# A two-layer attention and dense kernel: another order and another place of operands in the second product, and sums over the keys for two row tiles together

## Chip, cores and metric

The kernel runs on one core of a Trainium2 chip. The metric is the device time of one execution in microseconds (us); the median of three runs is given. The profile is that of one further execution. TensorE multiplies matrices, VectorE (DVE), ScalarE (ACT) and GpSimd (POOL) work element by element, SyncE (SP) issues the transfers.

## The reference

The input x has 2048 rows of D = 576 numbers. Twice in turn a linear attention and a dense block are added to it, each on a layer norm of x:

```python
qkv = x @ wqkv                                   # 32 heads of 18
phi_q = cat(softmax(q @ w_phi), softmax(-(q @ w_phi)))      # per head, 36 features
phi_k = cat(softmax(k @ w_phi), softmax(-(k @ w_phi)))
kv  = einsum("bhsf,bhsd->bhfd", phi_k, v)        # sums over all rows (keys)
z   = einsum("bhsf->bhf", phi_k)
o   = (phi_q @ kv) / (phi_q @ z + 1e-6)
x   = x + o @ wo
h   = relu(layernorm(x) @ w1 + b1) ** 2          # 576 -> 4608
x   = x + h @ w2 + b2                            # 4608 -> 576
```

All is in 32-bit floating point.

## The kernel before

**Tiling.** The rows are cut into NB = 4 blocks of TB = 512, each block into NT = 4 row tiles of P = 128. The 4608 hidden features are cut into NF = 36 slices of 128. For large products an operand is held as two parts, a high part (rounded to fp32r by ScalarE) and a low part (the difference, by VectorE or GpSimd); a product is then high x high + low x high + high x low. Such a product is one pass of TensorE per pair of parts.

**The dense block of a single block of rows** (`g_mlp`, from L1093; two blocks in each layer, so four in all). `first(f)` loads a slice of w1 and of w2 (r1, r2), splits them (h1 and l1; s2), and takes a PSUM tile ph. `hidden(f)` runs 14 matmuls of 512 columns into ph (L1135). `square(f)` makes the squares on ScalarE and their low part on VectorE (hh, hl in the tile hb, which begin SK = 48 numbers, 192 bytes, into it). The second product has two kinds of matmul. `by_rows` (L1162) handles the first R = D - P = 448 output columns: squares of one row tile are the weights, w2's first 448 columns are the moving operand, and each row tile t has its own accumulator acc[t]. `features` (L1153) handles the last 128 output columns the other way round: w2's last 128 columns are the weights, 512 squares are the moving operand, and the accumulator acc[KC] is transposed at the end. `second(f)` runs, for slice f, 12 matmuls of the first kind and 3 of the second. A step of the loop is first(f + 1), hidden(f), square(f), second(f - 1).

The tile s2 holds r2's high part in columns 0 to 575 and its low part in columns 576 to 1151: within a low or high part the first 448 columns are for by_rows, the last 128 for features. It is filled by one activation (L1114) and two subtractions (L1119 on VectorE, L1120 on GpSimd). It has room for 1440 columns.

**The pair of blocks** (`g_pair`, from L1380). The other two blocks of a layer go through the hidden product together, by a scheme of seven products for two slices (`product`, L1461, weights made by `split_pair`). For the first of the two the second product runs in between (`products`: by_rows L1493, features L1483); the squares of the second are kept in memory and its second product comes at the end (`seconds`). Here `second` already runs all 12 row matmuls and then the three of the features. `load_wide` (L1449 to L1451) fills s2 as above.

**The sums over the keys.** `kv_tile` (L670) adds one row tile's share of kv and z into a PSUM tile kvp that lives through a layer: for each of the 32 heads a matmul with 32 columns of values as weights in a 128 x 32 part of the array and 36 moving columns (L686); the profile counts two matmuls for each, 64 for a row tile. It reads the values (tiles of four slots, `next_slot`) and the softmaxes e (buffers of the tag "E", four of them). In layer 0 `g_keys` makes values, keys and softmaxes tile by tile for three blocks and sums a tile when two newer ones are waiting (`pending`); the last two of them are summed in `g_k` by `then`. In layer 1 `back_keys` makes the keys of two blocks beside `seconds` of layer 0 (`late` holds what isn't summed yet: a tile is summed when one newer one waits, the last one when the next block starts), and after it a third block's tiles are summed one by one behind their values (`lagged`, L1888). The last block's four tiles are summed in `barrier` (L1667): `keys()` makes the values of tile t + 2 and sums tile t, and between its steps the query softmaxes (`softs`) and the queries of another block go on.

**Order.** The program's text gives priorities: within a basic block a scheduler at compile time puts each engine's instructions in order by their place in the text and by when buffers and operands are ready; `tc.issue_after` pins some behind others. `weave` puts steps of one generator between those of another by costs written in the program. A tile's buffer is given to the next tile of its tag when the last reader is done.

Of the kernel before, what the change touches and what calls it, by code (L numbers as in the profile page):

```python
# [7 lines left out]
F32 = mybir.dt.float32  # L8
# [13 lines left out]
def layers_kernel(  # L22
# [42 lines left out]
    NS = H // NQ  # L65
    PAD = 32
    SK = 48
    assert VW <= 32 and NS == HG + 1 and NG == NQ + 1

    cst = ctx.enter_context(tc.tile_pool(name="cst", bufs=1))  # L70
# [28 lines left out]
    def drain(gen):  # L99
        for _ in gen:  # L100
            pass
# [655 lines left out]
    def g_k(x, pair, es, name, then=None, ready=None):  # L757
        raws = []
        for t in range(NT):
            for i in range(t, min(t + 2, NT)):  # L760
                if i == len(raws):
                    raws.append(make_raw(x, i, pair, f"{name}k"))
                    yield
            if ready and t == 2:
                ready()
            with tc.issue_after(dense["split", 0].ins) if ready and t == 2 else nullcontext():
                es.append(soft_k(raws[t], f"{name}K{t}"))
            if then and t:
                then(t - 1)
            yield  # L770
        if then:
            yield
            then(NT - 1)
            yield
# [318 lines left out]
    def g_mlp(layer, b, x, after, name, rest=None, then=None):  # L1093
# [7 lines left out]
        def first(f, early=False):  # L1101
            cols = slice(f * P, (f + 1) * P)
            r1 = sb.tile([P, NC, P], F32, tag="r1", name=f"{name}r1_{f}")
            r2 = sb.tile([P, D], F32, tag="r2", name=f"{name}r2_{f}")
            nc.sync.dma_start(r1[:, :KC], w1[: KC * P, cols].rearrange("(c p) n -> p c n", p=P))
            load_twice(r1[:, KC], w1, f * P, P)
            nc.sync.dma_start(r2, w2[cols])
            hl1 = sb.tile([P, NC * HP], F32R, tag="h1", name=f"{name}h1_{f}")
            h1 = hl1[:, : NC * P].rearrange("p (c n) -> p c n", n=P)
            l1 = hl1[:, NC * P : 2 * NC * P].rearrange("p (c n) -> p c n", n=P)  # L1110
            s2 = sb.tile([P, NC * HP], F32R, tag="s2", name=f"{name}s2_{f}")
            with tc.issue_after(dense["turn", 2 * f + 1].ins) if early else nullcontext():
                nc.scalar.activation(h1, r1, AF.Copy)
            nc.scalar.activation(s2[:, :D], r2, AF.Copy)  # L1114
            with tc.issue_after(dense["scaled1"].ins) if early else nullcontext():
                dense["lowered"] = (nc.gpsimd if early else nc.vector).tensor_sub(l1, r1, h1.bitcast(F32))

            def low():
                nc.vector.tensor_sub(s2[:, D : D + R], r2[:, :R], s2[:, :R].bitcast(F32))  # L1119
                nc.gpsimd.tensor_sub(s2[:, D + R : 2 * D], r2[:, R:], s2[:, R:D].bitcast(F32))  # L1120

            if early:
                lows.append(low)
            else:
                low()
            ph = wtile(f"{name}ph{f}") if f == 1 else ps_a.tile([P, TB], F32, tag="h", name=f"{name}ph{f}")
            parts[f] = (h1, l1, s2, ph)
# [19 lines left out]

        def features(f, ks):
            s2, hh, hl = parts[f]
            hi, lo = s2[:, R:D], s2[:, D + R : 2 * D]  # L1150
            for k in ks:
                a, m = ((hi, hh), (lo, hh), (hi, hl))[k]
                nc.tensor.matmul(acc[KC], a, m, start=(f == 0 and k == 0), stop=(f == NF - 1 and k == 2))  # L1153

        def by_rows(f, ts, ks):
            s2, hh, hl = parts[f]
            hi, lo = s2[:, :R], s2[:, D : D + R]
            for t in ts:
                rows = slice(t * P, (t + 1) * P)
                for k in ks:  # L1160
                    a, m = ((hh, hi), (hh, lo), (hl, hi))[k]
                    nc.tensor.matmul(acc[t][:, :R], a[:, rows], m, start=(f == 0 and k == 0),  # L1162
                                     stop=(f == NF - 1 and k == 2))

        def second(f):

            for ks in ((0, 1), (2,)):
                by_rows(f, range(NT), ks)
                features(f, ks)
            del parts[f]  # L1170

        every = slice(0, TB)
# [207 lines left out]
    def g_pair(layer, blocks, x, after, name):  # L1380
# [61 lines left out]
        def load_wide(f):  # L1442
            if f >= NF and f % 2:
                r2 = sb.tile([P, NC, P], F32, tag="r1", name=f"{name}r2_{f}").rearrange("p c n -> p (c n)")[:, :D]
            else:
                r2 = sb.tile([P, D], F32, tag="r2", name=f"{name}r2_{f}")
            nc.sync.dma_start(r2, w2[(f % NF) * P : (f % NF + 1) * P])
            s2 = sb.tile([P, NC * HP], F32R, tag="h1" if f >= NF and f % 2 else "s2", name=f"{name}s2_{f}")
            nc.scalar.activation(s2[:, :D], r2, AF.Copy)  # L1449
            nc.vector.tensor_sub(s2[:, D : D + R], r2[:, :R], s2[:, :R].bitcast(F32))  # L1450
            nc.gpsimd.tensor_sub(s2[:, D + R : 2 * D], r2[:, R:], s2[:, R:D].bitcast(F32))  # L1451
            wide[f] = s2

        def product(k, ps, key, op, start):
# [22 lines left out]
        def features(f, ks):  # L1477
            b, g = divmod(f, NF)
            s2, (hh, hl) = wide[f], high[f]
            hi, lo = s2[:, R:D], s2[:, D + R : 2 * D]  # L1480
            for k in ks:
                a, m = ((hi, hh), (lo, hh), (hi, hl))[k]
                nc.tensor.matmul(accs[b][KC], a, m, start=(g == 0 and k == 0), stop=(g == NF - 1 and k == 2))  # L1483

        def by_rows(f, ts, ks):
            b, g = divmod(f, NF)
            s2, (hh, hl) = wide[f], high[f]
            hi, lo = s2[:, :R], s2[:, D : D + R]
            for t in ts:
                rows = slice(t * P, (t + 1) * P)  # L1490
                for k in ks:
                    a, m = ((hh, hi), (hh, lo), (hl, hi))[k]
                    nc.tensor.matmul(accs[b][t][:, :R], a[:, rows], m, start=(g == 0 and k == 0),  # L1493
                                     stop=(g == NF - 1 and k == 2))
# [172 lines left out]
    def barrier(layer, b, prev, x, xprev, kes, vpair, qpair):  # L1667
# [13 lines left out]
        def keys():  # L1681
            for t in range(NT):
                if t + 2 < NT:
                    vts.append(make_v(x, t + 2, vpair, f"{n}"))
                with tc.issue_after(ahead[0].ins) if ahead else nullcontext():
                    kv_tile(layer, vts[t], kes[t], f"{n}{t}")
                yield

        softs = g_soft(raws, er, f"{n}f", 2)
# [55 lines left out]
    keep_split("k", kpair)  # L1745
    pending = []

    def g_keys(b):
        for t in range(NT):
            vt = make_v(xT[b], t, vpair, f"v0_{b}")  # L1750
            raw = make_raw(xT[b], t, kpair, f"k0_{b}")
            yield
            e = soft_k(raw, f"K0_{b}_{t}")
            if len(pending) > 1:
                kv_tile(0, *pending.pop(0))
            pending.append((vt, e, f"kv0_{b}_{t}"))
            yield
        if b < NB - 2:
            spill(b, xT[b])

    for b in range(NB - 1):
# [2 lines left out]
    load_biases()  # L1764
    kes = []
    qpair = []
    drain(g_k(xT[NB - 1], kpair, kes, f"k0_{NB - 1}", then=lambda t: pending and kv_tile(0, *pending.pop(0)),
              ready=lambda: qpair.extend(wpair("q", "t0", TAGS_B))))

    order = [NB - 1, NB - 2] + list(range(NB - 2))  # L1770
# [2 lines left out]
    for layer in range(2):  # L1773
# [24 lines left out]
        def back_keys():  # L1798
            new_slots("vs")
            late, ahead = [], []  # L1800
            normed = {b: {} for b in order[:3]}

            def norm_of(b):
# [3 lines left out]
            for i, b in enumerate(order[:3]):  # L1807
# [8 lines left out]
                    if n > 5:  # L1816
                        next(loads, None)
                drain(loads)
                while late:
                    kv_tile(1, *late.pop(0))  # L1820
                    yield 0.8
                if not last:
                    spill(b, xk)
                    norm = norm_of(order[i + 1])
# [18 lines left out]
                        raw_half(t, half)  # L1843

                def start(t):
                    es[t] = soft_parts(raws.pop(t), f"k{m}K{t}")

                def end(t):
# [3 lines left out]
                def keep_sums(t):  # L1852
                    if not last:
                        late.append((vts[t], es[t], f"kv{m}_{t}"))
                        if len(late) > 1:
                            kv_tile(1, *late.pop(0))

                for t in range(2):
                    raw_half(t, 0)
# [23 lines left out]
        if layer == 0:  # L1883

            prev, b = order[-2], order[-1]
            spare["tags"] = ["acc0", "acc1", "acc2", "acc3", "h"]
            x, xprev, vpair = {}, keep["x"], keep["v"]
            weave(lagged(NT, lambda t: make_v(xprev, t, vpair, "v1_prev"),  # L1888
                         lambda t, vt: kv_tile(1, vt, keep["es"][t], f"kv1_prev{t}")),
                  g_norm(lambda t: rows[t], x, "n1_last"), 1.0)  # L1890
            kpair = wpair("k", "w1_last", TAGS_B)
            kes = []
            qpair = []
            drain(g_k(x, kpair, kes, "k1_last", ready=lambda: qpair.extend(wpair("q", "t1", TAGS_B))))
            order = [b, prev] + order[:2]
# [22 lines left out]
```

## Time and profile before

| | before |
|---|---|
| median of three runs | 2455.33 us (2454.56 to 2456.44) |
| profiled execution, its own time | 2458.63 us |
| its span, first to last instruction | 2456.9 us |
| granted TensorE clock | 1.000 |
| matmuls in the profile | 15110 |
| DMA traffic | 348.67 MB, mean 142 GB/s |

PE is TensorE's matmuls, PEld its loads of weights. In the timeline a line has the start in us, the time to the end of the last instruction of a group, the engine, the line of the kernel, operation, output tile <- input tiles, shape of weights, shape of the moving operand and the number of instructions. A name such as m_3acc is block 3's accumulator; m_p stands for the pair, t0 for the barrier of layer 0. Matmuls are pipelined, so the time of one (362 or 389 ns) is longer than the distance between the starts of two, and that distance is the cost of one in a stream. In the groups by shape a line ends with the busy time in us and mean ns of one, then the idle time of the engine before it and what ended that.

### The profile page before, as it was taken

The numbers are of one execution on the slowest core, as the hardware profiler recorded it, in microseconds if no ns is written. First come the engines' busy times: TensorE is split into PE (matmuls) and PEld (weight loads), VectorE is DVE, ScalarE is ACT, GpSimd is POOL, SyncE is SP. The second block draws the span as 40 slices with busy tenths as digits, with TensorE's granted clock in tenths as the row PEclk, the third lists the DMA queues.
The fourth block names the chain that finished last, engine by engine and source line by source line (L and its number), as shares of the span: only waits on it lengthen the run. The fifth ranks groups of instructions, "written<-read, shape, count | busy, mean of one in ns | idle before, by whom it ended". The sixth has DMA issues, their size and how long they took to land. (4 is left out here: it accounts for less than half of the span.)

```text
span 2456.9 us, 41466 instructions
## 1 busy us (share of the span) xinstructions
PE 2444.1 (99%) x15110; PEld 2168.8 (88%) x15110; DVE 1534.4 (62%) x2503; ACT 1261.0 (51%) x2243; POOL 967.4 (39%) x1117
## 2 busy tenths in 40 slices
PE   9999999999999999999999999999999999999999
PEld 8999888889888888888999998888888888888898
DVE  7778939464866655545766787584547665555454
ACT  4344545443546766664433445554445466666643
POOL 4455303212335565542433442132122455565322
PEclk9999999999999999999999999999999999999999
DMA  9224533356434433338753154333573444433364
GB/s 325 72 73 165 164 101 98 102 162 218 135 119 139 146 109 107 112 101 299 252 190 143 54 173 121 104 98 114 159 242 94 128 137 146 122 96 118 114 198 129
DMA packets 248891, 348.67 MB, mean 142 GB/s; under 512 B 30126, under 2 KB 155950, under 8 KB 246126
## 3 DMA queue, kind: packets, MB, share of 16 engines
q1 hardware_dynamic: 247428, 344.66, 44.6%
q8 instruction: 118, 1.93, 0.3%
q10 hardware_dynamic: 1258, 1.37, 0.2%
q14 instruction: 87, 0.71, 0.1%
HBM read 280.93 MB, written 65.00 MB: 141 GB/s over the span
## 5 line engine op out<-in xcount | busy, mean ns | idle before, releaser
L1451 POOL TENSOR_TENSOR m_ps<-m_pr,m_ps 128x128 fp32r<-128x128 f32 x144 | 122.1, 848 | 317.5 <-ACT m_ps L1449 262.3
L1450 DVE TENSOR_TENSOR m_ps<-m_pr,m_ps 128x448 fp32r<-128x448 f32 x144 | 101.2, 703 | 181.4 <-ACT m_ps L1449 181.4
L1493 PE MATMUL m_pacc<-m_ps,m_phb 128*128 128x448 f32 x864 | 185.1, 362 | 0.0
L1493 PEld LDWEIGHTS m_pacc<-m_ps,m_phb 128*128 128x128 f32 x864 | 161.9, 188 | 14.7
L1449 ACT ACTIVATE m_ps<-m_pr 128x576 fp32r<-128x576 f32 x144 | 98.3, 683 | 119.6 <-issue 68.0
L1493 PE MATMUL m_pacacc<-m_ps,m_phc 128*128 128x448 f32 x648 | 147.2, 365 | 0.0
L1493 PEld LDWEIGHTS m_pacacc<-m_ps,m_phc 128*128 128x128 f32 x648 | 119.4, 188 | 7.9
L1162 PE MATMUL m_2acc<-m_2s,m_2hb 128*128 128x448 f32 x432 | 99.6, 364 | 0.0
L1162 PE MATMUL m_0acc<-m_0s,m_0hb 128*128 128x448 f32 x432 | 99.5, 364 | 0.0
L1162 PE MATMUL m_3acc<-m_3s,m_3hb 128*128 128x448 f32 x432 | 98.9, 364 | 0.0
L1162 PE MATMUL m_1acc<-m_1s,m_1hb 128*128 128x448 f32 x432 | 98.9, 364 | 0.0
L1135 PE MATMUL m_2ph<-a_2nh,m_2h 128*128 128x512 f32 (+1 forms) x380 | 97.4, 383 | 0.1
L1135 PE MATMUL m_0ph<-a_0nh,m_0h 128*128 128x512 f32 (+1 forms) x380 | 97.3, 383 | 0.1
L1135 PE MATMUL m_1ph<-t1onh,m_1h 128*128 128x512 f32 (+1 forms) x380 | 96.8, 382 | 0.0
L1135 PE MATMUL m_3ph<-t0onh,m_3h 128*128 128x512 f32 (+1 forms) x380 | 96.8, 382 | 0.0
L1162 PEld LDWEIGHTS m_2acc<-m_2s,m_2hb 128*128 128x128 f32 x432 | 80.9, 188 | 10.1 <-ACT m_2hb L1143 0.2
L1162 PEld LDWEIGHTS m_0acc<-m_0s,m_0hb 128*128 128x128 f32 x432 | 80.9, 188 | 10.0 <-ACT m_0hb L1143 0.2
L1162 PEld LDWEIGHTS m_3acc<-m_3s,m_3hb 128*128 128x128 f32 x432 | 81.0, 188 | 9.8
L1162 PEld LDWEIGHTS m_1acc<-m_1s,m_1hb 128*128 128x128 f32 x432 | 81.0, 188 | 9.8
L1120 POOL TENSOR_TENSOR m_3s<-m_3r,m_3s 128x128 fp32r<-128x128 f32 x36 | 25.0, 696 | 161.4 <-ACT m_3s L1114 154.0
L1120 POOL TENSOR_TENSOR m_1s<-m_1r,m_1s 128x128 fp32r<-128x128 f32 x36 | 25.3, 704 | 160.5 <-ACT m_1s L1114 145.8
L1135 PEld LDWEIGHTS m_1ph<-t1onh,m_1h 128*128 128x128 f32 x380 | 68.7, 188 | 13.8 <-DVE t1onh L517 0.2
(2448 smaller groups left out, 7294.6 us busy)
## 6 DMA issues: line engine op xcount, KB each, us to landing
m_pr<-in_B_w SPq DMA_DIRECT2D x144, 288.0 KB
m_pr<-in_B_w SPq DMA_DIRECT2D x72, 256.0 KB
hd<-m_pu SPq DMA_DIRECT2D x72, 256.0 KB
m_pg<-hd SPq DMA_DIRECT2D x72, 256.0 KB
m_3r<-in_B_w SPq DMA_DIRECT2D x36, 288.0 KB
m_2r<-in_B_w SPq DMA_DIRECT2D x36, 288.0 KB
m_1r<-in_B_w SPq DMA_DIRECT2D x36, 288.0 KB
m_0r<-in_B_w SPq DMA_DIRECT2D x36, 288.0 KB
```

The lines of the kernel that those rows point to most:

```text
L1120: nc.gpsimd.tensor_sub(s2[:, D + R : 2 * D], r2[:, R:], s2[:, R:D].bitcast(F32))
L1135: dense["hidden"] = nc.tensor.matmul(ph[:, cols], a, m, start=(k == 0), stop=(k == len(ops) - 1))
L1162: nc.tensor.matmul(acc[t][:, :R], a[:, rows], m, start=(f == 0 and k == 0), stop=(f == NF - 1 and k == 2))
L1449: nc.scalar.activation(s2[:, :D], r2, AF.Copy)
L1450: nc.vector.tensor_sub(s2[:, D : D + R], r2[:, :R], s2[:, :R].bitcast(F32))
L1451: nc.gpsimd.tensor_sub(s2[:, D + R : 2 * D], r2[:, R:], s2[:, R:D].bitcast(F32))
L1493: nc.tensor.matmul(accs[b][t][:, :R], a[:, rows], m, start=(g == 0 and k == 0), stop=(g == NF - 1 and k == 2))
```

## The change

In s2 the parts are set out anew: rows' high part at column 0, rows' low part at 448, features' high part at FC = 2 x 448 + 48 = 944, features' low part at 1072. The activation that filled the high part becomes two. `second` of `g_mlp` runs the features' three matmuls together behind all twelve of the rows. And kv_tile is called for two row tiles together: in `g_keys` when three are waiting, in `g_k` for both that are left, in `barrier` and for the third block of layer 1 behind every second tile; in `back_keys` all that is waiting, which by the order of its pipeline is four tiles when the next block starts.

```diff
+    FC = 2 * (D - P) + SK
...
-            nc.scalar.activation(s2[:, :D], r2, AF.Copy)
+            nc.scalar.activation(s2[:, :R], r2[:, :R], AF.Copy)
+            nc.scalar.activation(s2[:, FC : FC + P], r2[:, R:], AF.Copy)
...
-                nc.vector.tensor_sub(s2[:, D : D + R], r2[:, :R], s2[:, :R].bitcast(F32))
-                nc.gpsimd.tensor_sub(s2[:, D + R : 2 * D], r2[:, R:], s2[:, R:D].bitcast(F32))
+                nc.vector.tensor_sub(s2[:, R : 2 * R], r2[:, :R], s2[:, :R].bitcast(F32))
+                nc.gpsimd.tensor_sub(s2[:, FC + P : FC + 2 * P], r2[:, R:], s2[:, FC : FC + P].bitcast(F32))
...
-            hi, lo = s2[:, R:D], s2[:, D + R : 2 * D]
+            hi, lo = s2[:, FC : FC + P], s2[:, FC + P : FC + 2 * P]
...
-            hi, lo = s2[:, :R], s2[:, D : D + R]
+            hi, lo = s2[:, :R], s2[:, R : 2 * R]
...
             for ks in ((0, 1), (2,)):
                 by_rows(f, range(NT), ks)
-                features(f, ks)
+            features(f, range(3))
```

The same edits of s2, features and by_rows stand in `g_pair`. The sums:

```diff
                 with tc.issue_after(ahead[0].ins) if ahead else nullcontext():
-                    kv_tile(layer, vts[t], kes[t], f"{n}{t}")
+                    for i in (t - 1, t) if t % 2 else ():
+                        kv_tile(layer, vts[i], kes[i], f"{n}{i}")
...
+    def sum_pending():
+        for _ in range(min(2, len(pending))):
+            kv_tile(0, *pending.pop(0))
...
-            if len(pending) > 1:
-                kv_tile(0, *pending.pop(0))
+            if len(pending) > 2:
+                sum_pending()
...
-    drain(g_k(xT[NB - 1], kpair, kes, f"k0_{NB - 1}", then=lambda t: pending and kv_tile(0, *pending.pop(0)),
+    drain(g_k(xT[NB - 1], kpair, kes, f"k0_{NB - 1}", then=lambda t: sum_pending(),
...
-                while late:
-                    kv_tile(1, *late.pop(0))
-                    yield 0.8
+                if late:
+                    sum_late()
+                    yield 1.6
...
                 def start(t):
+                    if len(late) > 1:
+                        sum_late()
                     es[t] = soft_parts(raws.pop(t), f"k{m}K{t}")
...
                     if not last:
                         late.append((vts[t], es[t], f"kv{m}_{t}"))
-                        if len(late) > 1:
-                            kv_tile(1, *late.pop(0))
...
-            weave(lagged(NT, lambda t: make_v(xprev, t, vpair, "v1_prev"),
-                         lambda t, vt: kv_tile(1, vt, keep["es"][t], f"kv1_prev{t}")),
-                  g_norm(lambda t: rows[t], x, "n1_last"), 1.0)
+            def prev_sums():
+                made = {}
+                for t in range(NT + 1):
+                    if t < NT:
+                        made[t] = make_v(xprev, t, vpair, "v1_prev")
+                    for i in (t - 2, t - 1) if t and t % 2 == 0 else ():
+                        kv_tile(1, made.pop(i), keep["es"][i], f"kv1_prev{i}")
+                    yield
+
+            weave(prev_sums(), g_norm(lambda t: rows[t], x, "n1_last"), 1.0)
```

`sum_late` sums all that `late` holds.

More of the change, by code (lines that the diff above doesn't have):

```diff
@@ L1448, in load_wide @@
             s2 = sb.tile([P, NC * HP], F32R, tag="h1" if f >= NF and f % 2 else "s2", name=f"{name}s2_{f}")
-            nc.scalar.activation(s2[:, :D], r2, AF.Copy)
-            nc.vector.tensor_sub(s2[:, D : D + R], r2[:, :R], s2[:, :R].bitcast(F32))
-            nc.gpsimd.tensor_sub(s2[:, D + R : 2 * D], r2[:, R:], s2[:, R:D].bitcast(F32))
+            nc.scalar.activation(s2[:, :R], r2[:, :R], AF.Copy)
+            nc.scalar.activation(s2[:, FC : FC + P], r2[:, R:], AF.Copy)
+            nc.vector.tensor_sub(s2[:, R : 2 * R], r2[:, :R], s2[:, :R].bitcast(F32))
+            nc.gpsimd.tensor_sub(s2[:, FC + P : FC + 2 * P], r2[:, R:], s2[:, FC : FC + P].bitcast(F32))
             wide[f] = s2
@@ L1479, in features @@
             s2, (hh, hl) = wide[f], high[f]
-            hi, lo = s2[:, R:D], s2[:, D + R : 2 * D]
+            hi, lo = s2[:, FC : FC + P], s2[:, FC + P : FC + 2 * P]
             for k in ks:
@@ L1487, in by_rows @@
             s2, (hh, hl) = wide[f], high[f]
-            hi, lo = s2[:, :R], s2[:, D : D + R]
+            hi, lo = s2[:, :R], s2[:, R : 2 * R]
             for t in ts:
@@ L1800, in back_keys, with sum_late @@
             late, ahead = [], []
+            def sum_late():
+                while late:
+                    kv_tile(1, *late.pop(0))
             normed = {b: {} for b in order[:3]}
```

## The prediction

> **What bounds the kernel now.** I read the page first, for the engines' shares.
>
> ```profile
> span 2456.9 us, 41466 instructions
> PE 2444.1 (99%) x15110; PEld 2168.8 (88%) x15110; DVE 1534.4 (62%) x2503; ACT 1261.0 (51%) x2243; POOL 967.4 (39%) x1117
> ```
>
> TensorE is busy all the time, and the next engine has a third of its time free. A change gains here only by what it takes out of TensorE's stream, and loses only by what holds that stream up. Busy says little about speed, so I went to the timeline of TensorE, where the distance from one start to the next is the cost of a matmul. One step of a block that runs alone (hidden product of one slice of features, second product of the slice before):
>
> ```profile
> 420.71 1.31 PE L1135 MATMUL m_3ph<-t0onh,m_3h 128*128 128x512 f32 x5
> ...
> 423.93 1.76 PE L1162 MATMUL m_3acc<-m_3s,m_3hb 128*128 128x448 f32 x8
> 425.53 0.63 PE L1153 MATMUL m_3acc<-m_3hb,m_3s 128*128 128x512 f32 x2
> 426.00 0.98 PE L1162 MATMUL m_3acc<-m_3s,m_3hb 128*128 128x448 f32 x4
> 426.81 0.39 PE L1153 MATMUL m_3acc<-m_3hb,m_3s 128*128 128x512 f32 x1
> 427.05 1.31 PE L1135 MATMUL m_3ph<-t0onh,m_3h 128*128 128x512 f32 x5
> ```
>
> From start to start: 14 hidden matmuls take 3.22 us (0.230 each), eight row matmuls 1.60 (0.200), two of the features 0.47 (0.235), four rows 0.81 (0.2025), one feature 0.24; 6.34 us in all. The same shapes elsewhere are cheaper. First the hidden product of an earlier step, then one step of the pair of blocks:
>
> ```profile
> 370.09 1.30 PE L1135 MATMUL m_3ph<-t0onh,m_3h 128*128 128x512 f32 x5
> ...
> 373.26 1.76 PE L1162 MATMUL m_3acc<-m_3s,m_3hb 128*128 128x448 f32 x8
> ```
>
> ```profile
> 895.86 0.62 PE L1461 MATMUL m_ppx<-a_1nb11h,m_pwc_5h 128*128 128x512 f32 x2
> ...
> 905.39 2.56 PE L1493 MATMUL m_pacc<-m_ps,m_phb 128*128 128x448 f32 x12
> 907.79 0.86 PE L1483 MATMUL m_pacc<-m_phb,m_ps 128*128 128x512 f32 x3
> 908.50 0.62 PE L1461 MATMUL m_ppx<-a_1nt4h,m_pwc_5l 128*128 128x512 f32 x2
> ...
> 910.10 1.16 PE L1493 MATMUL m_pacc<-m_ps,m_phb 128*128 128x448 f32 x5
> ```
>
> The hidden product can run in 3.17 us (0.2264 each). The pair's 42 products up to 905.39 take 9.53 us (0.2269), its 12 rows 2.40 (0.200), its three features 0.71 (0.237). So the undisturbed prices are 0.227 for 512 columns and 0.200 for 448. By these a step of a single block would take 14 x 0.2265 + 12 x 0.200 + 3 x 0.227 = 6.25 us; it takes 6.34. The excess of 0.085 (between 0.08 and 0.09) is what parts of this change can reach: some 0.02 in the features, 0.02 in the four rows behind them, 0.045 in the hidden product behind the last feature. It begins each time with a feature matmul and outlasts it. The groups by shape say the same in mean durations:
>
> ```profile
> L1461 PE MATMUL m_ppz<-a_1nt1h,m_pwv 128*128 128x512 f32 x36 | 11.1, 389 | 0.0
> L1483 PE MATMUL m_pacacc<-m_phc,m_ps 128*128 128x512 f32 x216 | 61.9, 396 | 0.0
> L1153 PE MATMUL m_3acc<-m_3hb,m_3s 128*128 128x512 f32 x108 | 36.9, 397 | 0.0
> L920 PE MATMUL a_0pn<-a_0fl,kbh 126*126 126x512 f32 x16 | 6.3, 392 | 0.0
> ```
>
> Features are the slowest 512-column matmuls (396 and 397 against 389 ns). In the program before, the tiles of weights, of x and of squares begin at the same place within 128 bytes. Counted from there, hidden and pair products read weights and moving operand both at 0. The row passes read weights from the squares' tile at 192 + 512t (64 off) and move s2 at 0. The features read weights from s2 at 1792 and 4096 (0 off) and move squares at 192 and 2240 (64 off): the only steady 512-column product whose operands are 64 bytes apart. L920's weights stand at steps of 504 bytes, hence at all distances, and its mean lies between.
>
> **The change, part by part.** *Address.* With FC = 944 the features' weights stand at 3776 and 4288 bytes, 64 off like the squares that they meet, so both operands agree as in the pair's products. The rows' low part moves from 2304 to 1792, both multiples of 128: nothing. What it costs is one activation more per load:
>
> ```profile
> L1449 ACT ACTIVATE m_ps<-m_pr 128x576 fp32r<-128x576 f32 x144 | 98.3, 683 | 119.6 <-issue 68.0 <-PE m_pacc L1483 25.5 <-PE m_pacacc L1483 15.3
> L1417 ACT ACTIVATE m_pwa<-m_pr 128x384 fp32r<-128x384 f32 x36 | 18.9, 525 | 36.3 <-POOL m_pr L1432 29.0 <-POOL m_pr L1429 7.2
> ```
>
> 192 columns less cost 158 ns less, so 448 columns come to some 578 ns and 128 to 314: 0.21 us more per load, 288 loads, 60 us more on ScalarE (51 to 54%). VectorE's subtraction starts 0.1 us earlier, GpSimd's 0.2 later. The load runs a step of 6 us ahead, which hides this; uncovered it would be 0.2 us a load. I take 0.
>
> *Order.* In second(f), 35 steps in each of four blocks (140), the four rows with the low squares come straight behind the eight others, and the features follow in one run, as in the pair. The matmuls and their waits are the same; only which disturbs which changes.
>
> *Price of both.* I take it that features with equal operands run at 0.227, and that the last one, followed by weights at 0 off, still loses its 0.007 and disturbs what follows like the pair's features (908.50 to 910.10: 1.60 for seven, 0.02 over). Then 0.085 falls to 0.027 a step: 140 x 0.058 = 8.1 us. In the pair's first block (72 steps) 0.027 + 0.02 falls to 0.027: 1.4 us. In its second block the features are followed by rows:
>
> ```profile
> 1237.59 0.86 PE L1483 MATMUL m_pacacc<-m_phc,m_ps 128*128 128x512 f32 x3
> 1238.28 0.78 PE L1493 MATMUL m_pach<-m_ps,m_phc 128*128 128x448 f32 x3
> 1238.90 0.81 PE L589 MATMUL v_2pv<-w_2v1h,n_2h 128*128 128x288 f32 x5
> ```
>
> 0.69 and 0.62 against 0.68 and 0.60: 0.03 over, and now the weights that follow are 64 off like the last feature's moving squares, so all of it goes: 72 x 0.03 = 2.2 us. Sum 11.7. The ends: nothing of the disturbance is left, 140 x 0.085 + 72 x (0.047 + 0.03) = 17.4; or the longer one of the hidden product stays (0.045), 140 x 0.04 + 72 x 0.02 = 7.0.
>
> *Sums over the keys.* A row tile costs 64 narrow matmuls. One alone, then two that already stand together:
>
> ```profile
> 174.80 0.69 PE L589 MATMUL t0pv<-w0v1h,n_3l 128*128 128x288 f32 x4
> 175.33 0.82 PE L589 MATMUL t0pv<-w0v1l,n_3h 128*128 128x288 f32 x5
> 176.08 0.78 PE L686 MATMUL kvp<-k_3K0e,vslot 128*32 128x36 f32 x64
> 176.78 0.93 PE L589 MATMUL t0pv<-w0v0h,n_3h 128*128 128x288 f32 x5
> 177.55 0.70 PE L589 MATMUL t0pv<-w0v0h,n_3l 128*128 128x288 f32 x4
> ...
> 180.69 0.78 PE L686 MATMUL kvp<-k_3K1e,vslot 128*32 128x36 f32 x64
> 181.42 0.76 PE L686 MATMUL kvp<-k_3K2e,vslot 128*32 128x36 f32 x64
> ```
>
> Four projection matmuls take 0.53 (174.80 to 175.33), five then 0.66. Going in costs 176.08 - 175.33 - 0.66 = 0.09, the tile 0.70, coming out 177.55 - 176.78 - 0.66 = 0.11. The second tile of a run costs 0.73, so joining two saves 0.09 + 0.11 + 0.70 - 0.73 = 0.17. Before there are 30 runs (12 + 3 in layer 0; 8 + 4 + 3 in layer 1, two of them double). After it they are 6 + 2 and 2 + 2 + 2: in the second layer's keys under the pair a tile is only summed when the next block starts, four in a row. 16 runs fewer: 2.7 us (between 2 and 3.2, since other neighbours than projections occur).
>
> Holding a tile longer holds its buffer. In the barrier the values of the fourth row tile are made ahead of the first sum (3.9 us, now from 176.78 to 180.69), so it ends near 180.8 instead of 176.9, and VectorE and GpSimd wait for its buffer:
>
> ```profile
> 176.89 0.76 DVE L635 TENSOR_TENSOR t0fQ2e<-t0q3qs,t0fQ2m 128x576 f32<-128x576 f32 x1 [1.08 <-PE kvp L686]
> ...
> 199.38 1.35 DVE L835 TENSOR_TENSOR t0fQ1e<-t0fQ1e,t0fQ1r 128x576 f32<-128x576 f32 x1
> ```
>
> ```profile
> 201.32 0.27 PE L903 MATMUL t0opt<-ident,t0fQ1e 128*126 128x128 f32 x1
> ```
>
> Queued behind this subtraction on VectorE are the sums of the exponentials of the query tiles, from which t0fQ1e is scaled by 200.73; at 201.32, 0.6 us later, TensorE transposes it. If 4 us passed through, TensorE would stand 3.4 us in each of two barriers, 6.8; if the sums of the second query tile go ahead of the waiting subtraction (they need no new buffer), nothing. Those of the second tile are ready at about that time, and the sums over the keys, on which all the later steps hang, end no later than before; I take 0.5 us in all.
>
> *Sum.* 11.7 + 2.7 - 0.5 = 13.9 us. The profiled execution took 2458.6 us (span 2456.9 and 1.7 around it), 3.3 above the median of 2455.3; its sum gives 2444.7, and from the median **2441.4, say 2442**. With the ends of the prices this case reaches from 2435 (17.4 + 3.2) to 2449 (7.0 + 2.0, less 3 for half of the barriers' worst).
>
> **Rivals.** *The address is inert.* Row passes, too, have operands 64 bytes apart and run at 0.200, so the distance by itself does no harm; perhaps moving squares at 64 off are slow with any weights. Then features stay at 0.235 and only the order counts: of 0.085 a step 0.04 (short disturbance) to 0.065 (long) is left, 140 x 0.02 to 0.045 = 2.8 to 6.3 us, the pair gains nothing, and with 2.2 from the key sums it is 2447 to 2450. The Trainium skill ("SBUF — State Buffer", section "Who interferes with whom") gives TensorE two independent read ports, one for moving data and one for weights, and says that only the port pair shared by VectorE and GpSimd causes contention. By that rule this rival is the case; that equal shapes run at 0.227 and 0.237 here is not explained by it.
>
> *The disturbance only moves.* If the lost time belongs to the change of operand and not to the features (the four rows give 0.02 back, the hidden product gains it), only the key sums pay: 2455.3 - 2.2 = 2453, no change.
>
> *Slower.* Weights and moving data in the same line at the same time collide: then all 864 feature matmuls lose a further 0.007 and twice the disturbance follows in 284 steps: 6.0 + 284 x 0.02 = 11.7, less 2.2: 2465. It decides from a feature price of 0.240 on. Against it: the pair's products read both at 0 off and run at 0.227. With the barrier's 6.8 on top of "only moves" it would be 2460, also slower.
>
> **How the numbers follow.** About 0.2% (5 us) is what a measurement of this kernel can tell from no change. Forecast 0.57, address inert 0.20, only moves 0.15, slower 0.08. Nearly all of the forecast and most of the inert case are faster by over 5 us: 0.74. The rest of these and "only moves" are the same: 0.18; slower 0.08. The range from 2435 to 2451 leaves out "only moves", "slower" and little else.
>
> **What would show it.** Right: features of L1153 and L1483 at a mean near 389 to 392 ns, from start to start 0.69 or less for three; a single block's step at 6.28; runs of 128 narrow matmuls or more, 14 in all; four tiles in a row in the second layer's keys; no wait over 0.5 us at the first transposes behind the barriers. Wrong: features at 396, or a step still at 6.34 with the loss in the hidden product; TensorE waiting for VectorE behind the barriers; a wait for the new activation in the steps.

## The result, and the profile after

| | before | after |
|---|---|---|
| median | 2454.94 us (four runs) | 2468.83 us (2468.02 to 2469.42, four runs) |
| ratio | | 1.0052 (95%: 1.0040 to 1.0064) |
| profiled execution, its own time | 2458.63 us | 2468.67 us |
| granted clock | 1.000 | 0.997 |

The change makes the kernel 13.9 us slower, where 13 us less was forecast. The page of after, its span, the engines' shares and the queue that brings TensorE's instructions:

```profile
span 2466.9 us, 41912 instructions
...
PE 2438.9 (99%) x15110; PEld 2169.2 (88%) x15110; DVE 1527.7 (62%) x2503; ACT 1285.0 (52%) x2531; POOL 938.4 (38%) x1117
...
q8 instruction: 118, 1.93, 0.3%
```

TensorE has 15110 matmuls as before and is busy 5.2 us less than before (2444.1), in a span 10.0 us longer: it stands still for longer. So the change has two effects, and they are read in two places. First the steps that were to become cheaper, in the timeline of the same stretch and in the groups by shape:

```profile
418.45 1.31 PE L1137 MATMUL m_3ph<-t0onh,m_3h 128*128 128x512 f32 x5
...
421.67 2.56 PE L1164 MATMUL m_3acc<-m_3s,m_3hb 128*128 128x448 f32 x12
424.07 0.84 PE L1155 MATMUL m_3acc<-m_3hb,m_3s 128*128 128x512 f32 x3
424.75 1.31 PE L1137 MATMUL m_3ph<-t0onh,m_3h 128*128 128x512 f32 x5
```

```profile
L1486 PE MATMUL m_pacacc<-m_phc,m_ps 128*128 128x512 f32 x216 | 62.5, 400 | 0.0
L1486 PE MATMUL m_pacc<-m_phb,m_ps 128*128 128x512 f32 x216 | 60.8, 391 | 0.0
...
L1155 PE MATMUL m_3acc<-m_3hb,m_3s 128*128 128x512 f32 x108 | 30.4, 390 | 0.0
```

A step now takes 6.30 us (418.45 to 424.75) instead of 6.34: 3.22 for the hidden product, 2.40 for twelve row matmuls, 0.68 for three features. The features have fallen from 396 and 397 ns to 390 and 391 in the single blocks, and from 394 to 391 in the pair's first block. Those of its second block show 400, raised by stretches at half clock; in the version with single sums (first experiment), which has none there, they stand at 396 as before. Then where TensorE waits, in the table of waits after the start-up:

```profile
PE kvp L687 <- issue: 11.2, 4, 5.1
PE n_0p L510 <- DVE n_0l L505: 2.7, 1, 2.7
PE n_2p L510 <- DVE n_2l L505: 1.6, 1, 1.6
PE t0q2qp L590 <- DVE ko L733: 1.2, 1, 1.2
```

The columns are the total, how often, and the longest. "issue" is a wait for nothing that the profile shows. In the timeline its longest one stands in the middle of a row tile:

```profile
1211.44 0.76 PE L687 MATMUL kvp<-k_3K0e,vs 128*32 128x36 f32 x63
...
1212.56 0.38 PE L687 MATMUL kvp<-k_3K2e,vs 128*32 128x36 f32 x21
1218.06 0.87 PE L687 MATMUL kvp<-k_3K2e,vs 128*32 128x36 f32 x41 [5.12 <-issue]
...
1219.88 1.49 PE L1496 MATMUL m_pacacc<-m_ps,m_phc 128*128 128x448 f32 x3
1221.17 1.48 PE L1486 MATMUL m_pacacc<-m_phc,m_ps 128*128 128x512 f32 x3
```

Four tiles' 256 matmuls are in one run. They go 9 ns apart; after the 150th TensorE stands still for 5.3 us and then goes on with the same tile. K2e's softmax was ready: GpSimd had finished even K3e's by 1201.7. Behind the stop matmuls of 448 columns start 0.43 us apart (1219.88 to 1221.17, three) instead of 0.20. The windows show it too (window, length, busy time and count of PE, PEld, DVE, ACT and POOL, granted clock, DMA share, GB/s):

```profile
1160.00:1190.00 30.00, 30.00 (x197) 28.91 (x196) 18.92 (x26) 11.70 (x25) 10.97 (x12) 1.00 0.55 191
1190.00:1220.00 30.00, 23.21 (x359) 19.94 (x357) 25.33 (x43) 11.10 (x23) 14.84 (x17) 0.94 0.86 308
1220.00:1250.00 30.00, 30.00 (x181) 28.54 (x181) 5.61 (x8) 8.49 (x20) 2.82 (x4) 0.95 0.46 148
1280.00:1310.00 30.00, 24.45 (x375) 21.82 (x374) 17.55 (x24) 11.69 (x27) 8.73 (x8) 0.94 0.46 161
1400.00:1430.00 30.00, 26.89 (x433) 26.29 (x433) 21.36 (x37) 11.82 (x27) 11.07 (x8) 0.94 0.39 120
```

By the trace's clock records TensorE ran at half clock from 1216.4 to 1223.2, 1291.5 to 1294.9 and 1410.9 to 1414.4. Against the version with single sums (first experiment) after is 0.2 us late at the norm at 1131 us and 17.5 at 1429: the loss lies between, where the second layer's keys are summed. (In the first layer the barrier, with a wait of 1.4 us for VectorE, uses up the 2.0 us that the pairs have saved until then.)

### The profile page after: what moved, and what is told of

It reads as the page before. It is cut to its first block, busy times and chain, and to the rows that moved or that the text cites. A ratio compares the mean times of both kernels' runs of the same rounds, so it can differ in the third digit from the quotient of the medians.

```text
span 2466.9 us, 41912 instructions
## 1 busy us (share of the span) xinstructions
PE 2438.9 (99%) x15110; PEld 2169.2 (88%) x15110; DVE 1527.7 (62%) x2503; ACT 1285.0 (52%) x2531; POOL 938.4 (38%) x1117
## 3 DMA queue, kind: packets, MB, share of 16 engines
q8 instruction: 118, 1.93, 0.3%
## 5 line engine op out<-in xcount | busy, mean ns | idle before, releaser
L1454 POOL TENSOR_TENSOR m_ps<-m_pr,m_ps 128x128 fp32r<-128x128 f32 x144 | 99.8, 693 | 348.1 <-ACT m_ps L1452 324.8
L1453 DVE TENSOR_TENSOR m_ps<-m_pr,m_ps 128x448 fp32r<-128x448 f32 x144 | 95.0, 660 | 192.6 <-ACT m_ps L1451 191.7
L1451 ACT ACTIVATE m_ps<-m_pr 128x448 fp32r<-128x448 f32 x144 | 82.7, 574 | 123.7 <-issue 74.4
L1164 PE MATMUL m_2acc<-m_2s,m_2hb 128*128 128x448 f32 x432 | 93.7, 363 | 0.1
L1164 PE MATMUL m_0acc<-m_0s,m_0hb 128*128 128x448 f32 x432 | 93.7, 363 | 0.1
L1164 PE MATMUL m_3acc<-m_3s,m_3hb 128*128 128x448 f32 x432 | 93.3, 363 | 0.0
L1164 PE MATMUL m_1acc<-m_1s,m_1hb 128*128 128x448 f32 x432 | 93.3, 363 | 0.0
L1137 PEld LDWEIGHTS m_3ph<-t0onh,m_3h 128*128 128x128 f32 x380 | 68.8, 188 | 14.1 <-DVE t0onh L518 0.2
```

Of the source, the lines that this page charges most:

```text
L1137: dense["hidden"] = nc.tensor.matmul(ph[:, cols], a, m, start=(k == 0), stop=(k == len(ops) - 1))
L1451: nc.scalar.activation(s2[:, :R], r2[:, :R], AF.Copy)
L1453: nc.vector.tensor_sub(s2[:, R : 2 * R], r2[:, :R], s2[:, :R].bitcast(F32))
L1454: nc.gpsimd.tensor_sub(s2[:, FC + P : FC + 2 * P], r2[:, R:], s2[:, FC : FC + P].bitcast(F32))
```

## The experiments

**Theory A, instruction supply.** 1.93 MB in 118 packets on queue q8 are 16 KB each, one for 256 of TensorE's instructions: a matmul counts twice, with its weight load (15110 of each), and before's trace has 94 others. I counted, for each packet, how many instructions TensorE had begun when it started; k is the packet's number, from 0. In before and after no packet starts ahead of 256k + 152; in after three start only at 256k + 449, each in the middle of one of the stops. So a packet seems to be asked for at 152, and the stock ends at 449, 297 instructions or some 148 matmuls on. In products of 512 columns that is 34 us; in these sums, 9 ns a matmul, 1.3 us. In before a packet starts some 0.6 us (median) behind that point where other transfers move under 20 GB/s, and about 3 us where they move over 300; it takes 1.0 us. **Theory B**: operands come late, because norms and sums have changed places. **Theory C**: the new places or the new order cost something elsewhere.

### Sums and second product apart

Sums tile by tile as before, everything else as changed:

```diff
-                    for i in (t - 1, t) if t % 2 else ():
-                        kv_tile(layer, vts[i], kes[i], f"{n}{i}")
+                    kv_tile(layer, vts[t], kes[t], f"{n}{t}")
```

and likewise at the other four places.

> The changed kernel with the sums over the keys tile by tile again as before; the new places in s2 and the order of the second product stay. Theory A (instruction supply: a run of 256 narrow matmuls takes TensorE's 512 instructions in 2.4 us, faster than the next packet of instructions arrives, and the stop in the middle of the run is followed by half clock): the loss lies in the sums alone, the single block's step of 6.30 instead of 6.34 us is worth 140 x 0.04 = 5.6 us and the pair 1 to 2 us, so 2447 to 2449 us, and no stop over 2 us behind a kvp. Theory B (waits for operands: the norms of the second layer's keys are reached earlier, because the sums no longer stand ahead of them): the same time here, since the norms go back as well. Theory C (the new places or the order cost something elsewhere): above 2453.

Measured: 2450.46 us, ratio 0.9981 (0.9972 to 0.9989), 4.7 us less than before's 2455.14 beside it, and somewhat over the 2447 to 2449 expected. The reverse, before with the new sums alone:

> The kernel before with the sums for two and four tiles alone; s2 and the second product as before. A: 2455 plus the stops of the changed kernel (5.3 + 3.0 + 3.3 us inside runs of kvp, 1.7 + 2.9 us at the norms, 1.4 in the first barrier, some 4 us of half clock, less 2.2 saved): 2473 to 2477 us, stops at the same matmuls of the runs. B: the same total, with the stops wherever the operands come late. C: below 2462.

Measured: 2474.85 us, 1.0082 (1.0066 to 1.0097), with stops of 5.5, 3.1 and 3.4 us behind the same matmuls (the 150th, the 224th, the 33rd). The second product's part gains, the sums lose 18 to 20 us (2468.8 less 2450.5, 2474.9 less 2455.1); C falls.

### Which sums

Without the runs of four (one of three places, which all go back to before's text):

```diff
 def keep_sums(t):
     if not last:
         late.append((vts[t], es[t], f"kv{m}_{t}"))
+        if len(late) > 1:
+            kv_tile(1, *late.pop(0))
```

> The changed kernel with the second layer's keys under the pair summed as before (no four tiles in a row); two tiles together in the first layer, in both barriers and for the third block. A: the stops of 5.3 and 3.0 us and the waits of 1.7 and 2.9 us at the norms go; what is left is the second barrier, where two runs of two follow each other with little between, if the packet is late there too: 2447 to 2452 us. B: the waits at the norms go and the one inside the second barrier stays at 3.3 us: 2450 to 2452. C: above 2458.

Measured: 2454.87 us, 0.9999 (0.9990 to 1.0008): 14.0 less than after. Its waits:

```profile
PE kvp L687 <- issue: 3.7, 1, 3.7
PE t0q2qp L590 <- DVE ko L733: 1.2, 1, 1.2
```

The two stops and the two waits of the second layer's keys are gone; the second barrier's stop and the first barrier's wait for VectorE are left. The time lies over what A (2447 to 2452) and B (2450 to 2452) expected: both took the barriers' cost too low. Then the barriers too as before:

> As the one before, and the barriers also sum tile by tile as before; pairs are left in the first layer's keys and for the third block of the second layer, eight runs of two instead of sixteen single ones. A: a pair needs 256 instructions in 1.25 us, and there is more than that in hand when a packet is asked for: no stop over 1 us inside a run, and 8 x 0.17 = 1.4 us less than with single sums, 2446 to 2447 us. B: the same. If joining two tiles saves nothing, the time of the kernel with single sums.

Measured: **2447.97 us**, 0.9970 (0.9959 to 0.9981), 6.9 less than the last one, 2.5 less than with single sums, and the best of all, if 1 us over the 2446 to 2447 expected. The one wait of that kind that is left, and a run of two:

```profile
PE kvp L687 <- issue: 0.3, 1, 0.3
```

```profile
1333.95 0.77 PE L687 MATMUL kvp<-k_0K0e,vs 128*32 128x36 f32 x64
1334.57 0.76 PE L687 MATMUL kvp<-k_0K1e,vs 128*32 128x36 f32 x64
1335.26 0.66 PE L496 MATMUL n_lastp<-ident,n_lastn 128*128 128x128 f32 x4
```

Two tiles take 1.31 us (1333.95 to 1335.26). Joining pays, as long as the run stays short.

### Does the stop go with the count or with the data?

After, with 64 more small matmuls (128 instructions) at 15 us:

```diff
 nc.tensor.matmul(st["ps"][:, : 2 * NS * DH], ident[:1], zeros, start=True, stop=True)
+for _ in range(0 if layer else 32):
+    nc.tensor.matmul(st["ps"][:, : 2 * DH], ident[:1], zeros[:, 0], start=True, stop=True)
```

> The changed kernel with 64 more small matmuls (128 instructions, 36 zeros each) behind the zeroing of the first layer's sums at 15 us; nothing else. In the changed kernel TensorE stops behind the 150th of the 256 matmuls of the first run of four tiles and behind the 224th of the second. A (instruction supply, packets of 256 instructions counted from the program's start): the places move with the count, 64 matmuls on: behind the 214th of the first run, behind the 160th of the second (each 128 matmuls has one place where the stock ends, and the one that lies late in the run is the one that hurts). B (operands: the softmaxes or values come late): the stops stay at the 150th and the 224th. Time within 6 us of the changed kernel in both cases.

The first run, then the second, about the stop:

```profile
1223.62 0.39 PE L689 MATMUL kvp<-k_3K3e,vs 128*32 128x36 f32 x21
1228.97 0.93 PE L689 MATMUL kvp<-k_3K3e,vs 128*32 128x36 f32 x42 [4.96 <-issue]
```

```profile
1309.50 0.47 PE L689 MATMUL kvp<-k_2K2e,vs 128*32 128x36 f32 x31
1311.96 0.47 PE L689 MATMUL kvp<-k_2K2e,vs 128*32 128x36 f32 x32 [1.99 <-issue]
```

The stops are behind the 214th (three tiles and 22) and the 160th (two tiles and 32): both as A forecast, to the matmul. In the second barrier it moved from the 33rd to the 97th, 64 on as well. The data are the same, so B is out for the stops. The time, 2481.55 us (1.0107), is 12.7 over after, where 6 at most were expected; 9.4 of these lie ahead of the first barrier, where the extra matmuls are.

### The supply by itself

> No part of the layers: the output is a copy of x, and TensorE runs narrow matmuls of the kind of the sums on constants, first without traffic, then with 38 MB of loads beside it. Each time 64 wide matmuls of 512 columns, 768 narrow ones in a row, 64 wide ones, then pairs of tiles (128 narrow) with 0, 8, 8, 16, 16, 24, 24 wide ones ahead. A: the long run takes 9 ns a matmul for some 150 to 280 of them and then stops every 128: some 0.5 us without traffic (a packet starts 0.5 to 0.9 us after its request and takes 1.0, against 1.15 us for 128 matmuls), 2 to 5 us with traffic. Pairs with 16 wide ones ahead (3.6 us) do not stop without traffic, and stop for up to 2 us with it. B: 768 matmuls in a row take 7 us both times, without a stop.

The long run without traffic beside it but for the end of the copy, then with it:

```profile
24.71 1.42 PE L103 MATMUL pn<-e,vt 128*32 128x36 f32 x140
27.18 1.31 PE L103 MATMUL pn<-e,vt 128*32 128x36 f32 x128 [1.05 <-issue]
31.46 2.15 PE L103 MATMUL pn<-e,vt 128*32 128x36 f32 x128 [2.96 <-issue]
```

```profile
118.66 2.31 PE L103 MATMUL pn<-e,vt 128*32 128x36 f32 x247
125.64 2.15 PE L103 MATMUL pn<-e,vt 128*32 128x36 f32 x128 [4.67 <-issue]
132.39 2.14 PE L103 MATMUL pn<-e,vt 128*32 128x36 f32 x128 [4.60 <-issue]
```

After the first stop there is one every 128 matmuls to the end: 1.0 to 3.0 us without, 3.8 to 4.7 us with traffic (the "idle before"). (TensorE ran at half clock from 29.3 to 46.4 and from 124.9 to 155.6 us, so 128 matmuls take 2.15 us there instead of 1.3.) A pair behind 16 wide matmuls ran without a stop in the quiet part and stopped for 1.2 us under traffic. So these long runs were bound by their instructions with traffic and without; the stops of the quiet part were longer than the 0.5 us that A expected, and why stays open.

### What delays the packet, and spacing

The 2.3 MB that a norm's result sends to memory starts 0.2 and 1.3 us ahead of the first run of four. First the call was put behind the block's keys in the text:

> The changed kernel with one transfer moved: the 2.3 MB that a block's norm writes to memory while the first run of four tiles goes on are written at the end of the block's keys instead. A: with less traffic ahead of it the packet starts 1 to 2 us after its request instead of 4.5, so the stop inside the first run falls from 5.3 us to 2 to 3.5; the second run and the second barrier keep theirs (3.0, 3.3): 2465 to 2468 us. B: the stop stays at 5.3.

That told nothing: the transfer still began at 1211 to 1212 us (stop 4.9 us, 2468.67 us in all, 1.0053). So it was held back on SyncE's queue:

```diff
                         yield from paced(g_load("k", half, f"w{m}", wk), 0.3)
+                        if half == 0:
+                            with tc.issue_after(traced_on(nc.sync)):
+                                spill(b, xk)
```

> The changed kernel with the 2.3 MB of a block's norm held back on SyncE's queue behind the loads of that block's key weights (in the run meant for this, the transfer still began at 1211 to 1212 us, so it told nothing). Now they begin some 15 us behind the first run of four tiles. A with traffic as the cause of the delay: in that run the packet starts 1 to 2.5 us after its request instead of 4.0 to 4.5 and the stop falls from 5.3 us to 2 to 3.5; the second run (3.0) and the second barrier (3.3) as they were; 2464 to 2467 us. If the delay is not set by this traffic: the stop stays at 4.9 to 5.3 and the time at 2468 to 2469.

```profile
1213.64 0.38 PE L687 MATMUL kvp<-k_3K2e,vs 128*32 128x36 f32 x21
1216.85 0.57 PE L687 MATMUL kvp<-k_3K2e,vs 128*32 128x36 f32 x41 [2.83 <-issue]
```

The packet started 1.96 us behind the count of 152 instead of 4.45; the stop fell from 5.3 to 3.0 us, the others stayed (3.2, 3.5). 2465.34 us, 1.0039 (1.0025 to 1.0054). So this transfer makes up some 2.3 us of that stop. The rest is there without it, while other transfers still moved 198 GB/s (1208 to 1218 us; in after 346, 1209 to 1219 us). Spacing instead:

```diff
-                if late:
-                    sum_late()
+                while late:
+                    for _ in range(min(2, len(late))):
+                        kv_tile(1, *late.pop(0))
                     yield 1.6
```

> The changed kernel, but the four tiles that wait when the next block starts are summed as two and two with a step of the second product (15 matmuls of 0.2 us, 3.1 us) between. A: between the request and the end of the stock there are now 3 us more, against 4.5 + 1.0 us from request to landing at the first place and 1.9 + 1.0 at the second: the stop of 5.3 falls to 2 or less, that of 3.0 to 0.5 or less; the waits of 1.7 and 2.9 us at the norms stay, since the sums still stand behind them: 2461 to 2465 us. B: if the operands are late, the stops shrink by the 3.1 us as well, but the time stays, since the end is the same: 2468.

```profile
1212.89 0.87 PE L1496 MATMUL m_pacacc<-m_ps,m_phc 128*128 128x448 f32 x3
1213.60 0.87 PE L1486 MATMUL m_pacacc<-m_phc,m_ps 128*128 128x512 f32 x3
1214.40 0.34 PE L687 MATMUL kvp<-k_3K2e,vs 128*32 128x36 f32 x16
1219.01 0.95 PE L687 MATMUL kvp<-k_3K2e,vs 128*32 128x36 f32 x48 [4.28 <-issue]
```

2461.60 us, 1.0024 (1.0014 to 1.0033), as A forecast, but not by the path it gave. Only six matmuls, 1.5 us, came between, and the packet came as late as before, so the first stop is still 4.5 us; the second fell from 3.0 to 0.7, the norm's second wait, which was expected to stay, from 2.9 to 0.9, and the time at half clock there from 10.2 to 3.4.

### The second product: order, places, and a third place

Order alone, places alone, and, on top of the best version, squares that begin 256 bytes into their tile (`SK = 64` for 48; FC goes with it):

> The kernel before with one edit: in the single blocks the four row passes with the low squares come ahead of the three features; s2 and the sums as before. The places and the order together measured 4.7 us. If each does its own part (the prediction's sum): the four rows give back 0.02 a step and one start of the features is saved, 140 x 0.02 = 2.8 us, 2452 us, with the features still at 396 to 397 ns. If the order alone does it (the prediction's inert address): 2449 to 2451. If it only moves the loss into the hidden product: 2455.

> The kernel before with the new places in s2 alone, order and sums as before. If the place of the weights sets the features' price: features at 390 to 391 ns, 0.006 us less for each of 864, up to 5 us, of which the longer hidden product may take some back: 2450 to 2453 us. If the place is inert: 2455 and 396 to 397 ns.

> The best version so far (places, order, pairs in the first layer and for the third block: 2448.0 us) with the squares 256 bytes into their tile instead of 192, and the features' weights with them at 3840 and 4352: all operands of features, rows, hidden and pair products now begin on multiples of 128. If what is left of the excess (hidden product at 3.22 us behind the features instead of 3.17) comes from the change between operands 64 off and operands at 0, the hidden product goes to 3.17 and the step from 6.30 to 6.25: 140 x 0.05 + 72 x 0.02 = 8.4 us, 2440. If it comes from the change of kind (weights from s2, from squares, from h1) whatever the place: 2448. If rows whose weights and moving data both begin at 0 disturb each other: rows above 0.200 and the time above 2452.

A step with the order alone, then with squares at 256:

```profile
412.53 1.31 PE L1135 MATMUL m_3ph<-t0onh,m_3h 128*128 128x512 f32 x5
...
415.72 2.56 PE L1162 MATMUL m_3acc<-m_3s,m_3hb 128*128 128x448 f32 x12
418.12 0.86 PE L1153 MATMUL m_3acc<-m_3hb,m_3s 128*128 128x512 f32 x3
418.82 1.31 PE L1135 MATMUL m_3ph<-t0onh,m_3h 128*128 128x512 f32 x5
```

```profile
416.23 1.29 PE L1137 MATMUL m_3ph<-t0onh,m_3h 128*128 128x512 f32 x5
...
419.40 2.60 PE L1164 MATMUL m_3acc<-m_3s,m_3hb 128*128 128x448 f32 x12
421.84 0.86 PE L1155 MATMUL m_3acc<-m_3hb,m_3s 128*128 128x512 f32 x3
422.53 1.29 PE L1137 MATMUL m_3ph<-t0onh,m_3h 128*128 128x512 f32 x5
```

6.29 and 6.30 us, but made up otherwise: with squares at 256 the hidden product is at 3.17 (416.23 to 419.40) and the rows have gone from 2.40 to 2.44. Over all steps of a trace, what the matmuls lose against 0.2267 (512 columns) and 0.200 (448), from start to start, distances of 0.3 us and more left out, in us:

| | hidden | rows, single | features, single | pair: rows | pair: features | pair: products | sum | median time |
|---|---|---|---|---|---|---|---|---|
| before | 5.2 | 3.2 | 2.8 | 3.5 | 2.8 | 2.1 | 19.6 | 2455.3 |
| order | 3.6 | 0.9 | 2.9 | 3.5 | 2.8 | 2.1 | 15.8 | 2452.3 (0.9979 to 0.9997) |
| places | 5.5 | 2.8 | 2.8 | 2.8 | 1.9 | 2.0 | 17.8 | 2454.3 (0.9987 to 1.0005) |
| both, single sums | 5.3 | 0.8 | 0.3 | 2.7 | 1.8 | 2.0 | 13.0 | 2450.5 (0.9972 to 0.9989) |
| both, best sums | 5.3 | 0.7 | 0.4 | 2.8 | 1.9 | 2.0 | 13.0 | 2448.0 (0.9959 to 0.9981) |
| that, squares at 256 | 2.2 | 5.3 | 2.1 | 6.8 | 2.0 | 0.6 | 18.8 | 2453.0 (0.9983 to 1.0001) |

The sums agree with the times within what these can tell (the best version's further 2.5 us come from its pairs of tiles, which the table leaves out). Order alone takes the loss out of the rows and part of the hidden product; places alone only pay in the pair, and a single block's features stay at 396 to 398 ns; in a single block the features get cheap (0.3) with both, and the hidden product behind them gives part of it back. With all places on multiples of 128 the loss goes to the rows: of the three cases expected there, the third. The Trainium skill ("SBUF — State Buffer", section "Who interferes with whom") counts TensorE's two reads as independent; 5.8 us by the table, 5.0 by the medians, for a shift of operands by 64 bytes speak against taking that as "the place doesn't matter". What makes the place matter, no run here shows.

## Why the prediction was wrong, step by step

**The sums over the keys failed.** The step "joining saves 0.17 ... 30 runs to 14 ... 2.7 us" took a narrow matmul's price to be the same in a run of any length, and named the run of four without asking what feeds it. The saving is real and was put too low: the 0.73 taken for the second tile is the first tile of that pair (180.69 to 181.42), and eight runs of two brought 2.5 us instead of 1.4. But runs of four cost 14.0 us. Of these 5.3 + 3.0 are stops by supply; 1.7 + 2.9 are waits for VectorE at the norms, which TensorE reaches without the sums that before stood in front of them (this the trace shows, and no run isolates it); the remaining 1.1 us would be half clock (10.2 us of it in that stretch, partly within the stops) less what six joins save. The sign was in the trace of before, whose table of waits has, as its first line:

```profile
PE t1q0qp L589 <- issue: 1.1, 1, 1.1
```

It stands 4 us behind three tiles summed within as many (1394.3 to 1398.4), and its packet was the latest of all of before's, at 256k + 425. The prediction didn't ask what "issue" was.

**The barrier was mis-sized.** 0.5 us was taken of up to 6.8; the barriers cost 6.9. The chain foretold is there in the first: VectorE waits for the buffer,

```profile
176.93 0.76 DVE L636 TENSOR_TENSOR t0fQ2e<-t0q3qs,t0fQ2m 128x576 f32<-128x576 f32 x1 [4.44 <-PE kvp L687]
...
182.52 2.59 DVE L725 TENSOR_TENSOR kq<-kv,quarter 128x144 f32<-128x144 f32 x1
...
187.88 1.21 DVE L733 TENSOR_TENSOR ko<-kt,mask 126x504 f32<-126x504 f32 x2
```

its queue is late, `kq` and with it `ko` (187.88; in the best version 185.65), and TensorE waits 1.4 us for `ko` at 187.0, plus 0.35 at the first transposes. The prediction followed that queue to the transposes only. In the second barrier the 3.3 us are supply: two runs of two with 2.0 us of queries between. Instruction by instruction, the version without runs of four lies 2.3 us behind the best one ahead of the second barrier and 7.0 behind it, so the second barrier costs 4.7 of the 6.9: its stop (3.7 there) and the stretch at half clock.

**Price of both** was right in kind: in the single blocks features at 390 to 391 ns, three in 0.68, rows at 0.200. It was mis-sized: 6.6 by the table (4.7 by the medians), where 11.7 was forecast and 7.0 given as the lower end. That end's condition, the longer disturbance of the hidden product staying, is what happened (5.2 to 5.3 in the table). The single blocks brought 4.8 of 8.1, the pair 1.9 of 3.6, mostly because the features of its second block stayed at 396 ns. Nor were features the slowest 512-column matmuls of before: the pair's group m_ppx<-a_1nt4h,m_pwb, part of which stands right behind the features, had 401 ns, and it has 403 after, so there the loss stayed. The new activations cost ScalarE 24 us (1261.0 to 1285.0) instead of 60, and no wait for them shows. The inert address falls by the table (order alone 3.8, both 6.6, and the pair gained); by the medians the two lie only 1.8 us apart. "Only moves" is right for one part of the loss: squares at 256 moved it.

**Rivals.** "Slower" was there with a wrong mechanism: it wanted features at 0.240 us and more, and they became cheaper, so that its 2465 us lies near the 2468.8 measured is luck. And the bounds of the sums lacked one resource, TensorE's instructions, which the page lists only as a queue. With the sums as in the best version the forecast of 2442 would have been off by 6, not by 27.

## What to carry to other kernels

Before putting many short matmuls in a row, count instructions: here more than some 150 short matmuls without wide ones around them outran their packets, and each of the long stops cost 3 to 5 us and mostly a stretch at half clock besides. Runs of two tiles between wide work kept the saving in this kernel; under the 430 GB/s of the supply run even such runs stopped, for 1.0 to 2.6 us. A short "issue" wait in the middle of a stream is worth a look at the instruction queue, and a change of several parts is worth splitting: the best version is the change without its longest runs.

## What the runs showed of the hardware

- TensorE's instructions come in packets of 256, which seem to be asked for some 297 instructions before the stock ends. In before they start some 0.6 us behind that point (median, little other traffic), about 3 us under traffic, and 8.0 us in the longest case. The Trainium skill ("Runtime: NRT & Kernel Launch", section "Instruction fetch mechanics") has the same 16 KiB and 256 instructions, and says that crossing such a boundary is "mostly hidden"; that holds for this kernel's wide matmuls, and not for these, with stops up to 5.3 us.
- The same section of the Trainium skill gives TensorE room for 2048 instructions; the stops at 256k + 449 show a stock of about 300 behind the request.
- TensorE went on 1.2 to 1.4 us after the packet had landed (1216.86 to 1218.06; with the transfer held back, 1215.45 to 1216.85).
- With most stops and waits of 2.9 us and more went 3.4 or 6.8 us at half clock (the first began 3.6 us into its stop), but not with all: none with the 3.0 us from 1299.6 on.
